# Attention in units of 256 query rows on 64-row array tiles, ahead of a mixture-of-experts block

## The chip, the cores and the metric

The kernel runs on one core of a Trainium2 chip. The metric is the device time of one execution in microseconds (us), as the median of several runs. Five engines take part: TensorE (PE in the profile, with its weight loads as PEld), VectorE (DVE), ScalarE (ACT), GpSimd (POOL) and SyncE (SP), which here only issues DMAs. SBUF is the working memory with 128 partitions; PSUM takes what TensorE writes, in 8 banks of 2 KB per partition.

## The reference

```
# q, k, v: (4 batches, 8 heads, 576 positions, 64)
scores = q @ k.T / 8
heads 0..3: position i sees i-31 .. i                      ("L", local)
heads 4..7: position i sees every j <= i with j % 32 == i % 32   ("S", strided)
attn = exp(scores - max); attn /= attn.sum() + 1e-9
x = attn @ v                        # 2304 tokens x 512
e = argmax(x @ w_gate); weight = softmax probability of e
x = weight * (relu(x @ w1[e]) @ w2[e])   # 8 experts, 512 -> 1024 -> 512
y = silu(x @ w_in) @ w_out          # 512 -> 2048 -> 512
```

All inputs and the output are float32.

## The kernel before

The order of the work is written out by hand (`manual_schedule`): every engine takes its instructions in program order, and SyncE's DMAs too stand in that order.

**Attention** goes in units of up to 128 query rows, 11 per batch and 44 in all. An L unit has four tiles of 32 positions; each sees 64 keys, its own 32 and the 32 before. An S unit has two groups; a group is three residue classes of 18 positions, 54 rows padded to 64, and sees its own 54 keys. Each unit takes all four heads of its kind at once, as two pairs (`pr`). The two heads of a pair lie on partitions 0-63 and 64-127 of `q`. So that one matmul over all 128 partitions gives both heads, `kL`, `kS`, `vL` and `vS` have a doubled layout with zero blocks: head 0's keys stand in one half of the columns with zeros beneath, head 1's in the other half. GpSimd and VectorE write these zeros once for both sets of input buffers (`zeros`), and the data are loaded by one DMA for each half, onto 64 (or 54) partitions (`halves`, `loadL`, `loadS`).

A unit goes through these steps: `s_qk` adds a mask (L245, bf16 against an identity) and then the scores into one PSUM bank (L251 for L, 128x32 stationary and 128 columns; L258 for S, 128x64 and 108 columns; a float32 matmul stands in the trace as two MATMUL and two LDWEIGHTS records); `s_max`, `s_sub` (DVE), `s_exp` (ACT), `s_sum`, `s_eps`, reciprocal (DVE), `s_norm` (POOL multiplies P by the reciprocals); `s_tr` transposes the normalised P (L312) and copies it (ACT L316); `s_pv` multiplies by the values (L329), copies to `xr` (ACT L336) and writes `xr` to the DRAM buffer `xg` (SP L339, L345); `s_xt` transposes `xr` (L362) and copies it to `xT` (ACT L365, L371; one copy for each S group). Scores, transposes, and transposed outputs have two PSUM buffers each.

The main loop interleaves these steps: iteration i does `s_qk(i)`, `s_tr(i-3)`, `s_pv(i-4)`, `s_xt(i-5)`. When a batch has gone through `s_xt`, its gate goes into `extra`, one piece at a time: two times `g_l4` (L381), `g_lg` (L395), and small steps on DVE (`g_oh`).

**Input loads.** There are two sets of input buffers. Batch b+2 is loaded when batch b's L units, and later its S units, have been through `s_pv`; these issues stand on SP's queue among the writes to `xg`.

**Routing** follows the last gate: prefix sums on TensorE, a chain of small DVE steps, a permutation by matmuls (L598), then the first gather of rows from `xg`, and from there the experts (L828, L850) and the last MLP (L828, L920). Expert weights are loaded in the order of the experts' sizes (`raw`, L702), so their first load is issued when the routing has the order.

Of the kernel before, what the change touches and what calls it, by code (L numbers as in the profile page):

```python
# [37 lines left out]
def _constants():  # L38
# [10 lines left out]
    ok0[:32, :32] = False  # L49
    parts["mL0"] = np.where(ok0, 0, NEG).astype(f)  # L50
    parts["mL"] = np.where(ok, 0, NEG).astype(f)
    q = p % 64
    c = np.arange(54)
    oks = (q[:, None] // 18 == c[None, :] // 18) & (c[None, :] % 18 <= q[:, None] % 18)
    oks[q >= 54, 0] = True
# [32 lines left out]
def _program(nc, tc, top, order, qL, kL, vL, qS, kS, vS, wg, cst, wE, wM, out):  # L88
# [16 lines left out]
    with ExitStack() as ctx:  # L105
        io = ctx.enter_context(tc.tile_pool(name="io", bufs=1))
        cp = ctx.enter_context(tc.tile_pool(name="cp", bufs=1))
        wk = ctx.enter_context(tc.tile_pool(name="wk", bufs=4))
        psS = ctx.enter_context(tc.tile_pool(name="psS", bufs=2, space=PSUM))
        psT = ctx.enter_context(tc.tile_pool(name="psT", bufs=2, space=PSUM))  # L110
        psR = ctx.enter_context(tc.tile_pool(name="psR", bufs=1, space=PSUM))
        psX = ctx.enter_context(tc.tile_pool(name="psX", bufs=2, space=PSUM))
        psM = ctx.enter_context(tc.tile_pool(name="psM", bufs=1, space=PSUM))
# [3 lines left out]
        def C(n):  # L117
# [6 lines left out]
        mb = {n: cp.tile([128, 4, OFF[n][1]], BF16, name="b" + n) for n in ("mL", "mL0", "mS")}  # L124
# [6 lines left out]
        L4 = cp.tile([128, NT], F32, name="L4")  # L131

        shp = dict(
            qL=[128, 2, 576], kL=[128, 2, 2, 608], vL=[128, 2, 18, 2, 64],
            qS=[128, 2, 608], kS=[128, 2, 2, 594], vS=[108, 2, 11, 2, 64],
        )
        ins = [{n: io.tile(shp[n], F32, name=f"{n}{i}") for n in shp} for i in range(2)]

        def loadL(b):
            d = ins[b % 2]  # L140
            nc.sync.dma_start(out=d["qL"], in_=qL[b])
            for i in range(2):
                nc.sync.dma_start(out=d["kL"][64 * i : 64 * i + 64, :, i, :], in_=kL[b, 64 * i : 64 * i + 64])
            for i in range(2):
                nc.sync.dma_start(out=d["vL"][64 * i : 64 * i + 64, i], in_=vL[b, i])

        def loadS(b):
            d = ins[b % 2]
            nc.sync.dma_start(out=d["qS"], in_=qS[b])
            for i in range(2):  # L150
                nc.sync.dma_start(out=d["kS"][64 * i : 64 * i + 64, :, i, :], in_=kS[b, 64 * i : 64 * i + 64])
            for i in range(2):
                nc.sync.dma_start(out=d["vS"][54 * i : 54 * i + 54, i], in_=vS[b, i])

        def zeros(i, n):
            for h in range(2):
                p = slice(64 * h, 64 * h + 64)
                if n == "vS":
                    yield from (ins[i][n][:, h, x : min(x + 4, 11)] for x in range(0, 11, 4))
                elif n == "vL":  # L160
                    yield from (ins[i][n][p, 1 - h, x : x + 3] for x in range(0, 18, 3))
                else:
                    yield from (ins[i][n][p, x, 1 - h, :] for x in range(2))

        def halves(n, src, m, by, lo, hi):
            for i in range(2):
                o = d0[n][m * i : m * i + m]
                if by:
                    nc.sync.dma_start(out=o[:, :, i, lo:hi], in_=src[0, m * i : m * i + m, :, lo:hi])
                else:  # L170
                    nc.sync.dma_start(out=o[:, i, lo:hi], in_=src[0, i, :, lo:hi])


        d0 = ins[0]
# [4 lines left out]
        def warm(n):  # L179
            wt = psS.tile([128, 512], F32, tag="S", name="wt")  # L180
            for _ in range(n):
                nc.tensor.matmul(wt, zw[:, :128], zw, start=True, stop=True)
# [4 lines left out]
        nc.sync.dma_start(out=d0["qL"][:, :, :128], in_=qL[0, :, :, :128])  # L187

        halves("kL", kL, 64, 1, 0, 288)
        nc.sync.dma_start(out=d0["qL"][:, :, 128:], in_=qL[0, :, :, 128:])  # L190
        halves("kL", kL, 64, 1, 288, 608)
        halves("vL", vL, 64, 0, 0, 12)
        for lo, hi in ((0, 336), (336, 608)):
            nc.sync.dma_start(out=d0["qS"][:, :, lo:hi], in_=qS[0, :, :, lo:hi])
            halves("kS", kS, 64, 1, lo, min(hi, 594))
            if lo == 0:
                halves("vL", vL, 64, 0, 12, 18)
        for z in zeros(0, "kL"):
            nc.gpsimd.memset(z, 0.0)
        nc.scalar.copy(idb, C("ident"))  # L200
        for n in ("mL0", "mL", "mS"):
            nc.scalar.copy(mb[n], C(n).unsqueeze(1).to_broadcast([128, 4, OFF[n][1]]))
        nc.scalar.copy(ident, C("ident"))
        for i, z in enumerate(zeros(0, "vL")):
            (nc.vector if i < 6 else nc.gpsimd).memset(z, 0.0)
        zl = [*zeros(0, "kS"), *zeros(1, "vS"), *zeros(1, "kL"), *zeros(1, "kS"), *zeros(1, "vL")]
        for z in zeros(0, "vS"):
            nc.vector.memset(z, 0.0)
        halves("vS", vS, 54, 0, 0, 11)
# [8 lines left out]
        for _ in range(6):  # L218
            nc.gpsimd.memset(zl.pop(0), 0.0)
# [98 lines left out]
        def s_pv(i):  # L318
# [27 lines left out]
            if b + 2 < B:  # L346
                if i % 11 == 4:
                    loadL(b + 2)
# [781 lines left out]
```

## Time and profile before

| | |
|---|---|
| median of 3 runs | 802.28 us (801.39 to 807.32) |
| profiled execution: its time | 804.88 us |
| its span, first to last instruction | 802.9 us |
| mean granted TensorE clock | 0.975 |
| PE / PEld / DVE / ACT / POOL busy | 760.1 / 664.8 / 437.7 / 350.2 / 214.9 us |

The busy shares are averages over two very different stages, the attention (up to about 125 us) and the experts with the MLP (from about 148 us), and have to be read by stage.

### The profile page before, as it was taken

What the parts mean: (1) busy time and instruction counts of PE and PEld (TensorE: products, weight loads), DVE (VectorE), ACT (ScalarE), POOL (GpSimd) and SP (SyncE); (2) the same over time, 40 slices, a digit from 0 to 9 for tenths busy, and PEclk for the clock granted to TensorE, in tenths of its full rate; (3) what the DMA queues carried; (4) which work ended last, traced back from release to release, by engine and by line L of the source; (5) the groups of instructions that cost most, each with busy time, mean ns of one, the idle gap of its engine ahead of it and who ended that gap; (6) DMA issues with size and microseconds to landing.
All of it is one profiled execution on the core that took longest, in us unless ns stands there. A gap on an engine that the chain in (4) does not pass through costs nothing.

```text
span 802.9 us, 13934 instructions
## 1 busy us (share of the span) xinstructions
PE 760.1 (95%) x4983; PEld 664.8 (83%) x4983; DVE 437.7 (55%) x979; ACT 350.2 (44%) x843; POOL 214.9 (27%) x272
## 2 busy tenths in 40 slices
PE   8788978899999999999999999999999999999996
PEld 4455644799988999999977899999999989999995
DVE  7444635775878888887899632232232233223221
ACT  4445644566656665674545432232232233223221
POOL 8412312653443444533366500010010000001001
PEclk8889988999999999999999999999999999999999
DMA  9986743866755856764222000010000000001001
GB/s 221 176 199 193 171 121 118 282 189 216 240 186 187 257 159 209 224 181 156 82 79 54 9 32 1 0 40 1 1 29 11 1 8 34 0 1 40 1 1 42
DMA packets 45309, 83.30 MB, mean 104 GB/s; under 512 B 7817, under 2 KB 14875, under 8 KB 44851
## 3 DMA queue, kind: packets, MB, share of 16 engines
q1 hardware_dynamic: 41896, 72.44, 31.9%
q0 software_dynamic: 3312, 9.91, 3.7%
q8 instruction: 41, 0.67, 0.4%
q14 instruction: 33, 0.27, 0.1%
q10 hardware_dynamic: 27, 0.01, 0.0%
HBM read 72.82 MB, written 9.52 MB: 103 GB/s over the span
## 4 chain that ended last, share of the span: by engine, by line
PE 69%; DVE 13%; DMA 10%; issue 4%; ACT 2%; POOL 1%; SPq 1%; ACTq 0%; POOLq 0%; DVEq 0%
PE hps L828 31%; PE acc L920 22%; PE acc L850 9%; DVE t L750 4%; DMA kS<-in_kS 3%; DMA vL<-in_vL 3%; DVE t L761 2%; DVE w L739 2%; PE XR L329 2%; DVE t L755 2%; DMA xg<-xr 1%; ACT w L738 1%; DMA raw<-in_wE 1%; DMA qS<-in_qS 1%; PE sc L258 1%
## 5 line engine op out<-in xcount | busy, mean ns | idle before, releaser
L828 PE MATMUL hps<-x,w 128*128 128x384 f32 (+7 forms) x1344 | 231.7, 321 | 6.1 <-DVE x L820 4.3
L828 PEld LDWEIGHTS hps<-x,w 128*128 128x128 f32 x1344 | 213.9, 188 | 13.2 <-DVE x L820 5.3
L936 DVE TENSOR_TENSOR g<-g,hps 128x384 f32<-128x384 f32 x96 | 53.1, 553 | 183.3 <-ACT g L935 183.3
L935 ACT ACTIVATE g<-hps 128x384 f32<-128x384 f32 x96 | 47.0, 490 | 179.0 <-PE hps L828 179.0
L850 PE MATMUL acc<-h,w 128*128 128x256 f32 (+7 forms) x768 | 120.0, 305 | 0.3 <-ACT yT L860 0.3
L850 PEld LDWEIGHTS acc<-h,w 128*128 128x128 f32 x768 | 112.5, 188 | 0.7 <-ACT yT L860 0.5
L920 PE MATMUL acc<-wm,h 128*128 128x512 f32 x432 | 109.1, 394 | 1.6 <-POOL h L938 1.6
L920 PE MATMUL acc<-w,h 128*128 128x512 f32 x432 | 107.0, 394 | 1.7 <-POOL h L938 1.7
L828 PE MATMUL hps<-x,wm 128*128 128x384 f32 x576 | 106.6, 336 | 0.0
L828 PEld LDWEIGHTS hps<-x,wm 128*128 128x128 f32 x576 | 101.8, 188 | 3.1
L949 POOL DMA_INDIRECT out<-ob,TI x18 | 17.6, 976 | 322.4 <-ACT ob L948 296.6
L920 PEld LDWEIGHTS acc<-w,h 128*128 128x128 f32 x432 | 80.2, 188 | 19.1 <-POOL h L938 3.8
L920 PEld LDWEIGHTS acc<-wm,h 128*128 128x128 f32 x432 | 80.0, 188 | 18.0 <-POOL h L938 3.7
L739 DVE TENSOR_TENSOR w<-raw,w 128x512 fp32r<-128x512 f32 x97 | 71.5, 765 | 29.9 <-ACT w L738 24.8
L937 ACT CAST h<-g 128x384 fp32r<-128x384 f32 x96 | 49.3, 513 | 66.7 <-DVE g L936 66.7
L738 ACT CAST w<-raw 128x512 fp32r<-128x512 f32 x128 | 73.0, 620 | 3.8 <-DVE nx L615 2.9
L938 DVE TENSOR_TENSOR h<-g,h 128x384 fp32r<-128x384 f32 x80 | 44.7, 559 | 46.3 <-ACT h L937 46.3
L739 POOL TENSOR_TENSOR w<-raw,w 128x512 fp32r<-128x512 f32 x31 | 44.5, 1436 | 26.2 <-ACT w L738 18.9
L269 DVE TENSOR_REDUCE mx<-sc 128x4 f32<-128x216 f32 (+3 forms) x44 | 17.5, 399 | 52.5 <-PE sc L258 34.3
L302 POOL TENSOR_TENSOR Pn<-P,rc 128x216 f32<-128x216 f32 (+3 forms) x43 | 24.8, 577 | 74.1 <-DVE rc L300 63.0
L777 POOL TENSOR_TENSOR wm<-raw,wm 128x256 fp32r<-128x256 f32 x32 | 24.0, 752 | 73.0 <-ACT wm L775 66.0
L750 DVE TENSOR_SCALAR t<-raw 128x256 uint32<-128x256 uint32 x64 | 42.6, 686 | 0.1
(151 smaller groups left out, 800.8 us busy)
## 6 DMA issues: line engine op xcount, KB each, us to landing
raw<-in_wE SPq DMA_DIRECT2D x128, 256.0 KB
raw<-in_wM SPq DMA_DIRECT2D x64, 256.0 KB
vL<-in_vL SPq DMA_DIRECT2D x6, 576.0 KB
vS<-in_vS SPq DMA_DIRECT2D x8, 297.0 KB
xg<-xr SPq DMA_DIRECT2D x40, 54.0 KB
xg<-xr SPq DMA_DIRECT2D x16, 128.0 KB
kL<-in_kL SPq DMA_DIRECT2D x6, 304.0 KB
qS<-in_qS SPq DMA_DIRECT2D x3, 608.0 KB
```

The lines of the kernel that those rows point to most:

```text
L302: (nc.gpsimd if i < N - 1 else nc.vector).tensor_tensor(out=v4(z["Pn"], r, w), in0=z["P"], in1=rc[:r].unsqueeze(2).to_broadcast([r, 4, w]) ...
L738: nc.scalar.copy(wh, raw)
L739: (nc.gpsimd if i % 4 == 0 and i != 8 else nc.vector).tensor_tensor(out=wl, in0=raw, in1=f32(wh), op=ALU.subtract)
L750: nc.vector.tensor_scalar(out=t, in0=hi, scalar1=3, scalar2=0x3FFFFFF8, op0=ALU.logical_shift_left, op1=ALU.bitwise_and,)
L777: nc.gpsimd.tensor_tensor(out=wl, in0=v, in1=f32(wh), op=ALU.subtract)
L828: nc.tensor.matmul(ps[:, :n], w[a][:, 128 * k : 128 * k + 128], xh[:, b, k, :n], start=i == 0, stop=i == 11)
L850: nc.tensor.matmul(acc[d][:, :n], w[a][:, 128 * d : 128 * d + 128], hc[:, b, :n], start=(f == 0 and a + b == 0), stop=(f == 7 and a == 1),)
L920: nc.tensor.matmul(acc[t], hc[:, a, 128 * t : 128 * t + 128], wt[b], start=(f == 0 and a + b == 0), stop=(f == 15 and a == 1),)
L935: nc.scalar.activation(g, ps[:, :n], AF.Sigmoid)
L936: nc.vector.tensor_tensor(out=g, in0=g, in1=ps[:, :n], op=ALU.mult)
L937: nc.scalar.copy(hc[:, 0, :n], g)
L938: (nc.gpsimd if first else nc.vector).tensor_tensor(out=hc[:, 1, :n], in0=g, in1=f32(hc[:, 0, :n]), op=ALU.subtract)
```

## The change

The unit is doubled: an L unit is eight tiles, an S unit four groups, 256 rows as two "columns" `s` of 128 rows; there are 9 L and 11 S units over all batches together, 20 in the order of a written list. The zero blocks and their memsets go. Each head has its own matmul on 64 array rows (`tile_position=(64*r, ...)`), with 64 score columns or 65 value columns; the two heads of a pair write to two PSUM banks (`sc[:, r]`, `X[:, r]`). The values get a column of ones, so that the sum of P comes out of `s_pv` as column 64; `s_sum` goes, P is transposed without being normalised, and `s_norm` (now on DVE, out of PSUM) normalises the result instead. K and V are loaded onto 128 partitions by one DMA each; there are three sets of input buffers. Scores, transposes, values' products and transposed outputs have one PSUM buffer each (the first and third of two banks), the gate has two. `xr` has 6 buffers instead of 14. The two zero writes to `tabd` go from SP's queue to GpSimd's. Routing, experts and MLP are the same, apart from which PSUM pools the routing uses.

```diff
-        wk = ctx.enter_context(tc.tile_pool(name="wk", bufs=4))
-        psS = ctx.enter_context(tc.tile_pool(name="psS", bufs=2, space=PSUM))
-        psT = ctx.enter_context(tc.tile_pool(name="psT", bufs=2, space=PSUM))
+        wk = ctx.enter_context(tc.tile_pool(name="wk", bufs=3))
+        psS = ctx.enter_context(tc.tile_pool(name="psS", bufs=1, space=PSUM))
         psR = ctx.enter_context(tc.tile_pool(name="psR", bufs=1, space=PSUM))
-        psX = ctx.enter_context(tc.tile_pool(name="psX", bufs=2, space=PSUM))
-        psM = ctx.enter_context(tc.tile_pool(name="psM", bufs=1, space=PSUM))
+        psT = ctx.enter_context(tc.tile_pool(name="psT", bufs=1, space=PSUM))
+        psX = ctx.enter_context(tc.tile_pool(name="psX", bufs=1, space=PSUM))
+        psM = ctx.enter_context(tc.tile_pool(name="psM", bufs=2, space=PSUM))
...
-            qL=[128, 2, 576], kL=[128, 2, 2, 608], vL=[128, 2, 18, 2, 64],
-            qS=[128, 2, 608], kS=[128, 2, 2, 594], vS=[108, 2, 11, 2, 64],
+            qL=[128, 2, 576], kL=[128, 2, 608], vL=[128, 18, 2, 65],
+            qS=[128, 2, 608], kS=[128, 2, 608], vS=[128, 11, 2, 65],
...
+        def load(b, n, lo=0, hi=None):
+            if n[0] == "v":
+                nc.sync.dma_start(out=ins[b % 3][n][:, lo:hi], in_=src[n][b, :, lo:hi])
+            else:
+                nc.sync.dma_start(out=ins[b % 3][n][:, :, lo:hi], in_=src[n][b, :, :, lo:hi])
...
+        load(0, "qL", 0, 256)
+        load(0, "kL", 0, 288)
+        load(0, "vL", 0, 8)
+        load(0, "qL", 256, 576)
+        load(0, "kL", 288, 608)
+        load(0, "vL", 8, 18)
+        load(0, "qS", 0, 280)
+        load(0, "kS", 0, 280)
+        load(0, "vS")
+        load(0, "qS", 280, 608)
+        load(0, "kS", 280, 608)
...
+        units = [("L", 0), ("L", 8), ("S", 0), ("S", 4), ("L", 16), ("S", 8)]
+        units += [("L", 24), ("L", 32), ("S", 12), ("S", 16), ("S", 20)]
+        units += [("L", 40), ("L", 48), ("S", 24), ("S", 28), ("S", 32)]
+        units += [("L", 56), ("L", 64), ("S", 36), ("S", 40)]
+        later = {
+            0: [(1, "qS"), (1, "kS"), (1, "vS")],
+            1: [(2, "qL"), (2, "kL"), (2, "vL")],
+            3: [(2, "qS"), (2, "kS"), (2, "vS")],
+            5: [(3, "qL"), (3, "kL"), (3, "vL")],
+            6: [(3, "qS"), (3, "kS"), (3, "vS")],
+        }
         N = len(units)
         st = {}
+        def parts(i):
+            ty, at = units[i]
+            if ty == "L":
+                return [(s, k, 32, *divmod(at + 4 * s + k, 18)) for s in range(2) for k in range(4)]
+            return [(s, k, 64, *divmod(at + 2 * k + s, 11)) for s in range(2) for k in range(2)]
...
+            sc = psS.tile([128, 2, 512], F32, tag="S", name="sc")
+            ps = parts(i)
+            starts = {s: k for s, k, m, b, t in ps if t == 0}
+            if ty == "S":
+                masks = [("mS", 0, 4)]
+            elif starts:
+                masks = [(["mL0", "", "mL2"][starts[s]] if s in starts else "mL", 2 * s, 2) for s in range(2)]
+            else:
+                masks = [("mL", 0, 4)]
+            for r in range(2):
+                for j, (m, c, n) in enumerate(masks):
+                    nc.tensor.matmul(
+                        sc[:, r, 64 * c : 64 * (c + n)].rearrange("p (a w) -> p a w", w=64), idb,
+                        mb[m].unsqueeze(1).to_broadcast([128, n, 64]), start=j == 0, stop=False,
+                    )
+            for s in range(2):
+                for pr in range(2):
+                    for s_, k, m, b, t in ps:
+                        if s_ != s:
+                            continue
+                        d = ins[b % 3]
+                        for r in range(2):
+                            h = slice(64 * r, 64 * r + 64)
+                            if ty == "L":
+                                q = d["qL"][h, pr, 32 * t : 32 * t + 32]
+                                kk = d["kL"][h, pr, 32 * t : 32 * t + 64]
+                            else:
+                                q = d["qS"][h, pr, 54 * t : 54 * t + 64]
+                                kk = d["kS"][h, pr, 54 * t : 54 * t + 64]
+                            c = 64 * (2 * s + pr)
+                            nc.tensor.matmul(
+                                sc[m * k : m * k + m, r, c : c + 64], q, kk,
+                                start=False, stop=s + pr == 2, tile_position=(64 * r, m * k),
+                            )
+            st[i] = dict(S=sc[:, :, :256].rearrange("p r (c w) -> p r c w", w=64))
...
+            z["D"] = wk.tile([128, 4, 2, 64], F32, tag="D", name="D")
             nc.vector.tensor_tensor(
+                out=z["D"].rearrange("p c r w -> p r c w"), in0=z["S"],
+                in1=z["mx"].unsqueeze(3).to_broadcast([128, 2, 4, 64]), op=ALU.subtract,
             )
         def s_exp(i):
             z = st[i]
+            z["P"] = wk.tile([128, 4, 128], F32, tag="P", name="P")
+            nc.scalar.activation(z["P"], z["D"].rearrange("p c r w -> p c (r w)"), AF.Exp, scale=0.125)
...
+        def s_tr(i):
             z = st[i]
+            z["T"] = psT.tile([128, 4, 128], F32, tag="T", name="T")
+            for c in range(4):
+                nc.tensor.transpose(z["T"][:, c, :], z["P"][:, c, :], ident)
+        def s_pt(i):
+            z = st[i]
+            z["PT"] = wk.tile([128, 4, 128], F32, tag="PT", name="PT")
+            nc.scalar.copy(z["PT"], z["T"])
+        def s_pv(i):
+            z = st[i]
+            ty, _ = units[i]
+            X = psR.tile([128, 2, 512], F32, tag="R", name="XR")
+            z["X"] = X[:, :, :260].rearrange("p r (c w) -> p r c w", w=65)
+            for s in range(2):
+                for pr in range(2):
+                    for s_, k, m, b, t in parts(i):
+                        if s_ != s:
+                            continue
+                        V = ins[b % 3]["v" + ty]
+                        for r in range(2):
+                            h = slice(64 * r, 64 * r + 64)
+                            c = 2 * s + pr
+                            nc.tensor.matmul(
+                                X[m * k : m * k + m, r, 65 * c : 65 * c + 65],
+                                z["PT"][h, c, m * k : m * k + m], V[h, t, pr, :],
+                                start=True, stop=True, tile_position=(64 * r, m * k),
+                            )
         def s_eps(i):
             z = st[i]
+            z["rc"] = wk.tile([128, 2, 4], F32, tag="rc", name="rc")
+            nc.vector.tensor_scalar_add(z["rc"], z["X"][:, :, :, 64], 1e-9)
+            nc.vector.reciprocal(z["rc"], z["rc"])
         def s_norm(i):
             z = st[i]
+            xr = z["xr"] = wk.tile([128, 2, 256], F32, tag="xr", name="xr", bufs=6)
+            nc.vector.tensor_tensor(
+                out=xr.rearrange("p s (q r w) -> p r (s q) w", q=2, r=2), in0=z["X"][:, :, :, :64],
+                in1=z["rc"].unsqueeze(3).to_broadcast([128, 2, 4, 64]), op=ALU.mult,
+            )
+        def s_put(i):
+            xr = st[i]["xr"]
+            ty, at = units[i]
+            if ty == "L":
+                nc.sync.dma_start(
+                    out=xg[32 * at : 32 * at + 256, 0:256].rearrange("(s p) d -> p s d", s=2), in_=xr
+                )
+                return
+            for k in range(2):
+                rows = [(s, m, b, t) for s, k_, m, b, t in parts(i) if k_ == k]
+                for s, m, b, t in rows:
...
+            z["XX"] = psX.tile([128, 4, 128], F32, tag="X", name="XX")
+            for c in range(4):
                 nc.tensor.transpose(
+                    z["XX"][:, c, :], z["xr"][:, c // 2, 128 * (c % 2) : 128 * (c % 2) + 128], ident
...
+        for i in range(N + 3):
             def on(j):
                 return 0 <= j < N
+            if on(i - 2):
+                s_eps(i - 2)
+                s_norm(i - 2)
+                s_put(i - 2)
             if on(i):
                 s_qk(i)
+            more()
+            if on(i - 1):
+                s_tr(i - 1)
+                s_pt(i - 1)
+            if on(i):
                 s_max(i)
+            more()
+            if on(i - 2):
+                s_xx(i - 2)
+            more()
             if on(i - 1):
+                s_pv(i - 1)
             if on(i):
                 s_sub(i)
+            more()
+            if on(i - 2):
+                s_xt(i - 2)
             if on(i):
                 s_exp(i)
+            for a in later.get(i, ()):
+                load(*a)
+            more(2)
```

## Rows read from the trace of the kernel before

**Rows 1.** Windows: length, busy us (instructions) per engine, granted clock, DMA share, GB/s.

```profile
0.00:44.00 44.00, 34.75 (x394) 20.05 (x394) 28.02 (x90) 20.76 (x65) 27.14 (x62) 0.84 0.96 196
125.00:148.00 23.00, 17.37 (x122) 9.65 (x122) 15.70 (x67) 8.88 (x27) 7.37 (x6) 0.85 0.52 163
148.00:803.00 655.00, 636.71 (x3636) 590.65 (x3634) 355.86 (x652) 276.61 (x609) 161.13 (x159) 1.00 0.28 88
```

**Rows 2.** Chain that ended last, to the first expert matmul: start, duration, what.

```profile
5.94 6.70 DMA vL<-in_vL
...
35.05 11.36 DMA kS<-in_kS
...
94.10 9.04 DMA qS<-in_qS
...
125.47 1.54 PE l L381 x16
...
147.64 4.51 PE hps L828 x36
```

**Rows 3.** The same chain: gate matmuls, then one unit's steps on TensorE.

```profile
78.09 0.96 PE l L381 x8
...
80.34 1.21 PE lg L395 x10
...
91.85 0.37 PE XX L362 x2
92.22 0.11 PE sc L245
92.33 0.57 PE sc L251 x16
92.91 0.36 PE T L312 x2
93.27 0.59 PE XR L329 x8
```

**Rows 4.** Windows: qS moving; kS and vS moving; only writes to xg.

```profile
67.00:68.00 1.00, 1.00 (x15) 0.76 (x13) 0.91 (x3) 0.50 (x3) 0.24 (x1) 1.00 1.01 363
69.00:72.00 3.00, 3.00 (x37) 1.81 (x36) 2.25 (x8) 1.96 (x7) 0.85 (x2) 1.00 0.94 235
...
111.00:115.00 4.00, 4.00 (x60) 2.84 (x61) 2.44 (x13) 1.94 (x7) 0.55 (x1) 1.00 0.22 66
```

**Rows 5.** Windows of L251 alone: PE busy (matmuls in flight), PEld, clock, DMA.

```profile
92.26:92.28 0.02, 0.02 (x3) 0.02 (x3) 1.00 0.00 0
92.28:92.30 0.02, 0.02 (x4) 0.02 (x6) 1.00 0.36 103
...
92.40:92.42 0.02, 0.02 (x8) 0.02 (x7) 1.00 0.00 0
```

**Rows 6.** The same for L329 of an S unit.

```profile
93.21:93.23 0.02, 0.02 (x2) 0.02 (x2) 1.00 0.19 51
93.37:93.39 0.02, 0.02 (x4) 0.02 (x4) 1.00 0.32 102
```

**Rows 7.** Groups by line and form up to 170 us: busy, mean ns, idle before.

```profile
L371 ACT COPY xT<-XX 128x108 f32<-128x108 f32 x40 | 10.6, 370 | 0.0
...
L251 PEld LDWEIGHTS sc<-kL,qL 128*32 128x32 f32 x288 | 8.6, 119 | 11.8 <-DMA xg<-xr 5.4 <-issue 3.6 <-POOL CUM L215 1.4
...
L295 DVE TENSOR_SCALAR rc<-sm 128x4 f32<-128x4 f32 x36 | 7.8, 216 | 0.0
...
L820 DVE TENSOR_TENSOR x<-xt,x 128x512 fp32r<-128x512 f32 x4 | 2.6, 670 | 1.0 <-ACT x L819 1.0
...
L819 ACT CAST x<-xt 128x512 fp32r<-128x512 f32 x4 | 2.2, 579 | 3.5 <-issue 3.5
```

**Rows 8.** Timeline of TensorE: the first score matmuls.

```profile
6.20 0.65 PE L251 MATMUL sc<-kL,qL 128*32 128x128 f32 x16 [1.07 <-DMA kL<-in_kL]
```

**Rows 9.** Window after a stall of TensorE: the granted clock.

```profile
47.00:51.00 4.00, 4.00 (x40) 1.59 (x36) 1.24 (x5) 1.43 (x4) 0.61 (x1) 0.50 1.01 216
```

More of the change, by code (lines that the diff above doesn't have):

```diff
@@ L131, in _program @@
         L4 = cp.tile([128, NT], F32, name="L4")
+        xT = cp.tile([128, 4, NT], F32, name="xT")
         shp = dict(
-            qL=[128, 2, 576], kL=[128, 2, 2, 608], vL=[128, 2, 18, 2, 64],
-            qS=[128, 2, 608], kS=[128, 2, 2, 594], vS=[108, 2, 11, 2, 64],
-        )
[L137 to L163, printed above, removed]
@@ L175, in _program @@
+        src = dict(qL=qL, kL=kL, vL=vL, qS=qS, kS=kS, vS=vS)
+        ins = [{n: io.tile(shp[n], F32, name=f"{n}{i}") for n in shp} for i in range(3)]
+        def load(b, n, lo=0, hi=None):
[3 more added lines that the diff above has]
+                nc.sync.dma_start(out=ins[b % 3][n][:, :, lo:hi], in_=src[n][b, :, :, lo:hi])
         zw = cp.tile([128, 512], BF16, name="zw")
@@ L186, in _program @@
         nc.sync.dma_start(out=cs[:, :nf], in_=cst[:, :nf])
[L187 to L199, printed above, removed]
-        nc.scalar.copy(idb, C("ident"))
[L201 to L209, printed above, removed]
+        load(0, "qL", 0, 256)
[9 more added lines that the diff above has]
+        load(0, "kS", 280, 608)
+        nc.scalar.copy(idb, C("ident"))
+        for n in ("mL0", "mL", "mS", "mL2"):
+            nc.scalar.copy(mb[n], C(n))
+        nc.gpsimd.tensor_copy(ident, C("ident"))
+        for n in ("qL", "kL", "vL"):
+            load(1, n)
         nc.sync.dma_start(out=cs[:, nf:], in_=cst[:, nf:])
         nc.sync.dma_start(out=wgs, in_=wg)
-        loadL(1)
         nc.gpsimd.memset(onb, 1.0)
@@ L215, in _program @@
         nc.gpsimd.memset(CUM[:, 0, :], 0.0)
[L216 to L228 removed]
+        nc.gpsimd.dma_start(out=tabd[0:PADF], in_=zt[:PADF])
@@ L352, in first_loads @@
-        def first_loads(i):
-            if i == 5:
-                loadS(1)
+        done = {"L": 0, "S": 0}
+        gated = [0]
         def s_xt(i):
             z = st.pop(i)
-            b, ty, t, n = units[i]
-            r = z["R"]
-            X = psX.tile([128, 2, 128], F32, tag="X", name="XX")
-            for pr in range(2):
-                nc.tensor.transpose(X[:, pr, :r], z["xr"][:r, 128 * pr : 128 * pr + 128], ident[:r, :r])
-            xT = xTs[b]
+            ty, at = units[i]
```

221 lines of the change are left out of this document (55 added, 166 removed).

## The prediction

> **What bounds the kernel now.** I read the windows by stage first [rows 1]. From 148 us on TensorE is busy 637 of 655 us at the full clock (granted 1.00, the 2.4 GHz level): experts and MLP are bound by TensorE, and the change leaves them alone. From 125 to 148 us runs the routing, a serial chain that starts at the last batch's gate, and it too stays. So the question is when the last gate starts: at 125.47 us now, and the first expert matmul follows at 147.64 [rows 2]. Whatever the attention gains comes out at the end one to one, as the first expert weights are requested by the routing's result and no attention buffer holds them up.
>
> Next comes the chain of waits up to there [rows 2]. Until 46 us it is made of input loads (kS from 35.05 lasts 11.36 us), and it meets qS again at 94.10 for 9.04 us. In the first 44 us the DMA engines are busy 0.96 of the time and deliver only 196 GB/s [rows 1]. Between these waits TensorE sets the pace: one unit takes .37 + .11 + .57 + .36 + .59 = 2.0 us [rows 3]. So the attention has two limits, the loads and TensorE, and the change touches both.
>
> **Loads.** With qS (128 partitions in one DMA) in motion the engines deliver 363 GB/s at full share; with kS and vS (64 and 54 partitions to a DMA) it is 235 at a share of .94 [rows 4]. After the change all loads have 128 partitions, so the bounds are 235 and 363. I take 330, near the row of the like shape. The amounts: per batch q 0.59 and 0.62 MB, k 0.62 each, vL 1.20, vS 0.73, together 4.4 MB, 17.8 MB with constants (zero blocks were never loaded, so bytes don't fall). A unit writes 0.26 MB to xg; alone, writes moved 66 GB/s at a share of .22, that is 300 at full share [rows 4].
>
> Where does TensorE wait? Unit 5 ("S", 8) is the first that needs batch 1's S data. Ahead of its scores stand 0.3 (constants) + 4.4 + 2.4 + 1.24 = 8.34 MB, 25.3 us at 330 GB/s, with an allowance of 2 us for the first issues and 0.8 MB of writes (2.6 us): 29.9 us. Later needs (unit 10, unit 15) come by the same sum some us ahead of their use. On SP's queue the writes of results now stand behind loads that wait for a free buffer or for the queue; `xr` has six buffers, so a write may be some five iterations (18 us) late before VectorE's normalisation, and with it TensorE, waits. I cost this at nothing; with slow loads it belongs to rival D.
>
> **TensorE.** The float32 matmuls are seen starting in groups: for L, four are in flight by 92.30, eight by 92.40 [rows 5], one group for each .11 us, four column tiles abreast; for S two abreast at about the same period [rows 6]. 16 records make four groups, .43 us, which with .14 of start and drain is the .57 of the chain [rows 3]. In the new units a matmul streams 64 or 65 columns instead of 108 or 128, so a group should take .055, but there are twice as many: 64 records (L) or 32 (S) in each of scores and values for 256 rows. No row shows two 64-row halves of the array at work together. If they do run together, eight (L) or four (S) are abreast and the streaming x is 8 x .055 = .44 us; if they add nothing, 16 x .055 = .88, which is what two units of before have. Weight loads count double also: one lasts 119 ns [rows 7], longer than a 55 ns matmul. A tile that loads one set while it works with the other then takes about (119 + 55) / 2 = 87 ns for a matmul, 8 x 87 = .70 us on eight tiles. S loads 64 columns at a time. I take x = .8.
>
> An iteration is then masks 2 x .11, four transposes .72, four more .74, twice the .15 around a segment, and 2x: 1.98 + 2x = 3.58 us, against 4.0 for two units of before. The other engines stay below it. VectorE: max, subtract and normalise with 512 elements each (.67 by L820 [rows 7]), two small steps (.2 each): 2.4. ScalarE: exponential and copy at .58 (L819), four copies for S at .37 (L371): 2.6. GpSimd loses its memsets and multiplications, which no chain row of before names, so this is worth nothing by itself. The single PSUM buffer for the scores costs nothing either: `s_qk(i+1)` waits for `s_sub(i)`, 1.4 us of VectorE, under the transposes and the values' matmuls (2.5 us) on TensorE; only the first iteration has nothing to cover it.
>
> **The sum.** Start as now, 6.2 us [rows 8] (fewer but larger first pieces). 20 iterations x 3.58 = 71.6. Three gates in between, each .96 + .96 + 1.2 = 3 [rows 3]: 9. Unit 5 could start at 6.2 + 5 x 3.58 = 24.1 and waits until 29.9: 5.8. After such a wait TensorE ran at half clock: at 47 to 51 us the granted clock was .50, the 1.2 GHz level, after it had idled [rows 9]; 3 us for that. Behind the last iteration the last unit still needs transposes .72, copy .58, values .95, reciprocal .4, normalisation .67, transposes .74, four copies 1.48, and some 10 hand-overs: 6.3. Together 101.9 us instead of 125.5, a gain of 23.6. The profiled span of 802.9 becomes 779.3 and its execution of 804.88 becomes 781.3; against the median of 802.28, which lies 2.6 lower, I predict 779.
>
> **Rivals.** A, *both halves abreast in full*: x = .44, the iteration 2.86, 57.2 for all; unit 5 would be ready at 20.5 and waits 9.4. Attention ends at 91: 768. For it: groups of four start within .04 us [rows 5]. Against it: the weight loads' length.
>
> B, *a price for each matmul whatever its width*: 16 matmuls now start within .4 us, 25 ns apart. If that is a floor, L costs 64 x 25 = 1.6 a segment and S .8; 9 x 5.18 + 11 x 3.58 = 86, the wait shrinks to 1: end at 108.5, time 785. Against it: three to four in flight within .04 us [rows 5], so starts stand closer together than 25 ns where tiles differ. The Trainium skill, in "TensorE: Matmul & The Clock Gate", Part 1, "Wait — 56ns, not 53.3ns?", states this floor of about 25 ns from start to start; here the rows contradict it across tiles. "TensorEngine Tiling (Array Packing)", "Instruction Overhead", speaks against the change too: one should not take a tiling factor from a dimension that is small already; no run here shows such narrow tiles yet.
>
> C, the other side, *weight loads that are not hidden*: the gate's second matmuls have 8 columns, so their weight loads stand bare: 1.21 / 10 = 121 ns for 128 columns [rows 3], 30 for 32, 60 for 64. If each 64-row load holds up its matmuls so, x = 64 x 30 ns = 1.94 for L and the same for S; iteration 5.86, all 117; no wait on loads is left, end at 139: 815, slower. It decides from x = 1.6 (25 ns for an L matmul, 50 for S), where 20 x 5.2 + 21.5 reaches 125.5. Against it: by 92.30 six loads are in flight beside four matmuls [rows 5]. For it: twice the loads for half the work each.
>
> D, *loads don't get faster*: at 235 GB/s batch 3's S data, needed by unit 15, are there at 17.8 MB / 235 = 75.7, + 11.4 (writes) + 2 = 89; five iterations, a gate and the tail make 116: 793. For it: the 54-partition and 64-partition rows mix with writes. Against: 363 GB/s with qS.
>
> That the change doesn't do what it says would show as x = .88 with loads as predicted: 782, inside the forecast.
>
> **How the numbers follow.** A measurement of this kernel can tell about 1% from no change: below 794 is faster, above 810 slower. Forecast 48% (772 to 787 with x between .6 and .95), A 14%, B 15%, C 12%, D 11%. The range leaves out C and the lower edge of A: 768 to 798. Faster: forecast, A, B and some over half of D less a margin for the unseen, .81; slower: most of C, .10; the rest, .09, between.
>
> **What would show it.** Right: in the windows, loads above 300 GB/s at full share in the first 40 us; one stall of TensorE near 25 to 30 us; iterations of 3.6 us; the last gate near 102 us; routing 22 us long as now. Matmul groups of L with more than four abreast speak for A; L iterations well longer than S ones for B; PEld busy without a gap through the scores and values for C. The forecast falls if TensorE is found waiting for VectorE or ScalarE in each iteration, if writes late on SP's queue hold up the normalisation, or if small matmuls leave the granted clock at .50.

## The result, and the profile after

The changed kernel takes 783.32 us (median of 4, 782.61 to 784.15), the kernel before 804.1 in the runs beside it (801.39 to 807.32): the ratio of the two is 0.974, its 95% interval 0.9696 to 0.9784. The prediction was 779, its range 768 to 798. The profiled execution took 783.98 us, its span 782.0.

Windows by stage (columns as in [rows 1]) of the changed kernel:

```profile
10.00:15.00 5.00, 0.00 (x0) 0.00 (x0) 0.00 (x0) 0.00 (x0) 0.00 (x0) 0.50 0.97 80
...
20.00:30.00 10.00, 7.44 (x196) 5.49 (x179) 3.50 (x8) 1.78 (x4) 0.00 (x0) 0.56 1.03 412
30.00:45.00 15.00, 9.95 (x325) 7.51 (x322) 7.22 (x15) 5.26 (x15) 0.84 (x2) 0.92 1.02 402
...
104.00:128.00 24.00, 16.89 (x115) 10.52 (x116) 16.63 (x68) 9.14 (x26) 7.28 (x6) 0.86 0.60 181
128.00:782.00 654.00, 636.08 (x3635) 590.48 (x3633) 355.75 (x651) 275.80 (x607) 159.75 (x159) 1.00 0.28 87
```

The experts' stage is the same to 0.6 us in TensorE's busy time (636.08 here, 636.71 in [rows 1]). The loads run at 400 to 412 GB/s from 20 to 45 us, where the kernel before had 196 in its first 44 us [rows 1]. But from 10 to 15 us no engine does anything, while the DMA engines are full and move 80 GB/s.

Chain that ended last (start, duration, what), with a steady stretch of an S and an L iteration:

```profile
3.91 12.67 DMA kL<-in_kL
...
40.16 2.76 issue
...
81.10 0.32 PE sc L226 x2
81.42 0.62 PE sc L245 x32
82.04 0.60 PE T L273 x4
...
82.73 0.59 ACT PT L278
...
83.36 0.70 PE XR L295 x32
84.06 0.33 PE sc L226 x2
84.39 0.84 PE sc L245 x53
...
87.56 0.79 PE sc L245 x53
...
104.39 1.17 PE l L372 x12
...
127.75 2.33 PE hps L812 x19
```

The chain reaches the last gate at 104.39 (125.47 in [rows 2]) and the experts at 127.75 (147.64), so the attention gives 21.1 us and the routing, 23.4 us long instead of 22.2, takes 1.2 back. (104.39 is where the last twelve of the gate's sixteen records begin; the other four begin at 103.40. Before, all sixteen stand together.) What the routing lost lies in its last steps on TensorE, from 124.31 on: they take 1.94 + 1.49 us at a mean granted clock of .55, close to the 1.2 GHz level, against 1.07 + .76 us at 1.00 before. By the end of the span the gain is 20.9 us (802.9 - 782.0). The S iteration from 81.10 to 84.06 takes 2.96 us and the next, up to the following mask at 87.24, 3.18; the forecast was 3.6. With steps that much faster, the last gate should have come before the forecast 101.9, not after it. The timeline of TensorE says where the rest went (the bracket holds the idle time ahead of the line and its releaser):

```profile
16.71 1.17 PE L245 MATMUL sc<-kL,qL 64*32 64x64 f32 x64 [7.75 <-DMA kL<-in_kL]
23.46 0.92 PE L245 MATMUL sc<-kS,qS 64*64 64x64 f32 x24 [1.70 <-issue]
29.82 0.33 PE L245 MATMUL sc<-kS,qS 64*64 64x64 f32 x4 [0.86 <-issue]
36.37 0.68 PE L295 MATMUL XR<-vS,PT 64*64 64x65 f32 x27 [1.46 <-issue]
42.92 0.43 PE L295 MATMUL XR<-vL,PT 64*32 64x65 f32 x6 [2.76 <-issue]
58.38 0.39 PE L385 MATMUL lg<-cs,L 128*128 128x8 f32 x2 [1.75 <-issue]
```

First a wait of 7.75 us of the second unit for its keys, a piece that was issued at 3.91 us. Then five gaps, 8.5 us together, each in the middle of a run of matmuls that had already begun. No semaphore ended them, which the profile calls "issue".

### The profile page after: what moved, and what is told of

Its sections match the earlier page's. It is cut to its first block, busy times and chain, and to the rows that moved or that the text cites. A ratio compares the mean times of both kernels' runs of the same rounds, so it can differ in the third digit from the quotient of the medians.

```text
span 782.0 us, 15274 instructions
## 1 busy us (share of the span) xinstructions
PE 730.9 (93%) x5897; PEld 657.3 (84%) x5899; DVE 423.9 (54%) x846; ACT 325.2 (42%) x738; POOL 173.2 (22%) x194
## 4 chain that ended last, share of the span: by engine, by line
PE 75%; DVE 11%; issue 5%; DMA 3%; ACT 2%; POOL 1%; SPq 0%; POOLq 0%; ACTq 0%; DVEq 0%
PE hps L812 32%; PE acc L904 22%; PE acc L834 11%; DVE t L734 3%; PE XR L295 2%; PE sc L245 2%; PE T L273 2%; DMA kL<-in_kL 2%; DMA raw<-in_wE 2%; DVE t L745 2%; DVE w L723 2%; DVE t L739 1%; ACT PT L278 1%; ACT w L722 1%; PE sc L226 1%
## 5 line engine op out<-in xcount | busy, mean ns | idle before, releaser
L761 POOL TENSOR_TENSOR wm<-raw,wm 128x256 fp32r<-128x256 f32 x32 | 24.2, 757 | 72.6 <-ACT wm L759 64.5
L750 DVE SCALAR_TENSOR_TENSOR raw<-m,t 128x256 f32<-128x256 bf16 x64 | 36.6, 592 | 1.2
L759 ACT CAST wm<-raw 128x256 fp32r<-128x256 f32 x32 | 13.0, 406 | 57.9 <-DVE raw L750 57.9
```

The costliest lines, as they stand in the source:

```text
L750: nc.vector.scalar_tensor_tensor(out=v, in0=m, scalar=TINY * TINY, in1=t.bitcast(F32), op0=ALU.is_ge, op1=ALU.mult)
L761: nc.gpsimd.tensor_tensor(out=wl, in0=v, in1=f32(wh), op=ALU.subtract)
```

## The experiments

Four theories: T1, the 7.75 us wait comes from the two zero writes to `tabd`, 224 rows of 4 bytes from 96 and 128 partitions, which the change put ahead on GpSimd's queue; T2, most of the gain is the loads' 128 partitions to a DMA; T3, the two halves of the array work abreast, and that is why the steps are shorter than forecast; T4, the gaps without a releaser come with the load traffic. One expectation has a T5: what the steps alone are worth in the kernel before. Rivals are named in each expectation. In the results, ratio and interval are those of the time to the kernel before. First what TensorE's steps are worth by themselves, then the waits.

**Heads in turn** (T3). All matmuls of the lower 64 rows first, then all of the upper, in scores and values:

```diff
-            for s in range(2):
+            for r_ in range(2):
+              for s in range(2):
...
-                        for r in range(2):
+                        for r in (r_,):
```

> The changed kernel with the order of the score and value matmuls changed: first all of the lower 64 array rows, then all of the upper, instead of the two in turn. Theory T3: the halves run together only when neighbours in the order lie on different halves; the 32 score records of an S unit then take .85 to .95 us instead of .62, the 64 of an L unit about .95 instead of .82 to .9; time 789 to 795. Rival: a matmul has a fixed price of about 10 ns (L) to 14 ns (S) whatever lies beside it, and the order means nothing: 783.

788.28 us (784.85 to 789.62), ratio 0.9774, interval 0.9743 to 0.9804. The chain of waits in this run, an S unit's scores and values and an L unit's scores:

```profile
83.31 0.33 PE sc L226 x2
83.63 0.91 PE sc L246 x30
...
85.22 0.59 ACT PT L279
85.86 0.98 PE XR L297 x30
...
87.16 0.92 PE sc L246 x60
```

The same 32 records (the chain counts 30 of them here) take .91 instead of .62 for the scores and .98 instead of .70 for the values; L's scores take .92 instead of .79 to .84. So the halves do work abreast when their matmuls alternate, nearly in full for S (.91 less .15 around it is .76; .62 less .15 is .47, and fully abreast would be .44) and only in part for L. One thing is not parted by this run: the two halves write to two PSUM banks, so matmuls that alternate between the halves alternate between the banks too. With that said, T3 holds in its mechanism. The time is just below the 789 to 795 expected of it. The trace gives a reason: beside the slower steps the gaps are 3.2 us together, where the changed kernel has 8.5.

**One batch loaded, the kernel before.** Only batch 0 is loaded, and all batches compute on its operands, so the output is another; only the time up to the last gate is read, since the experts then get other shares of the tokens.

```diff
-        loadL(1)
...
-            d = ins[b % 2]
+            d = ins[0]
...
-                if i % 11 == 4:
-                    loadL(b + 2)
-                if i % 11 == 10:
-                    loadS(b + 2)
+                pass
...
-            if i == 5:
-                loadS(1)
+            pass
```

> The kernel before in which only batch 0 is loaded and all 44 units compute on it (wrong output in batches 1 to 3, the end longer as experts overflow; only the time up to the last gate is read). Theory T5: without waits for loads TensorE's pace of 2.0 us a unit puts the last gate at 100 to 108 us, where the changed kernel with one batch has it at 94; so about 10 us of the change's work is in TensorE's steps. Rival: both come at the same time, 92 to 96, and the steps are worth nothing.

TensorE's timeline has the last gate at

```profile
103.16 1.61 PE L376 MATMUL l<-xT,wgs 128*32 128x288 f32 x16
```

as expected (100 to 108), and TensorE was busy all 80 us from 20 to 100. Of before's 125.47 us, 103.2 are steps and start, 22.3 waiting for loads and what follows from it.

**One batch loaded, the changed kernel.** The same edit there (also another output).

> The changed kernel in which only batch 0 is loaded and all 20 units compute on it (wrong output in batches 1 to 3; experts may then be fuller than their places and the end longer, so only the time up to the last gate is read). Theory T4: TensorE's gaps within a row of matmuls that nothing in the profile releases (1.7, .9, 1.5, 2.8 and 1.75 us, between 21 and 58 us) come from input loads that fill the DMA engines; without loads after 17 us they are gone (under 1 us in all), and so are the waits for data: after the first 17 us the last gate comes within some 65 us, at 80 to 85 us. Rival: the gaps are the price of twice as many TensorE instructions and stay: last gate at 88 to 95 us.

TensorE's timeline of this run:

```profile
16.92 1.17 PE L237 MATMUL sc<-kL,qL 64*32 64x64 f32 x64 [8.00 <-DMA kL<-in_kL]
24.31 0.92 PE L237 MATMUL sc<-kS,qS 64*64 64x64 f32 x24 [2.34 <-issue]
...
93.07 3.09 PE L364 MATMUL l<-xT,wgs 128*32 128x288 f32 x16
```

The last gate came at 93.07, not at T4's 80 to 85 but in the range that the rival had named, though not for the rival's reason, for the gaps did not stay: one of 2.34 us ended at 24.3 us, while batch 0 was still loading, and after it there were only two, of .20 and .36 us. T4 holds in this: the long gaps come with the traffic. The wait for the second unit's keys was 8.00 us as ever, so it has nothing to do with the later loads. It was still in the number, and the work behind it took 76 us and not the 65 that the expectation had reckoned.

**Zero writes late** (T1):

```diff
-        nc.gpsimd.dma_start(out=tabd[0:PADF], in_=zt[:PADF])
-        nc.gpsimd.dma_start(out=tabd[YC:TROWS], in_=zt[: TROWS - YC])
...
+            if i == 15:
+                nc.gpsimd.dma_start(out=tabd[0:PADF], in_=zt[:PADF])
+                nc.gpsimd.dma_start(out=tabd[YC:TROWS], in_=zt[: TROWS - YC])
```

> The changed kernel with one edit: the two writes of zeros to tabd (96 and 128 elements of 4 bytes), which GpSimd issues at 4.1 and 4.8 us, are issued in iteration 15. Theory T1: these writes are what slows every DMA between 10 and 16 us (33 to 73 GB/s there, second kL piece landing only at 16.7); without them the second unit's scores start by 9.5 us instead of 16.7, and the time falls by 5 to 8 us, to 775 to 778. Rival: the slow stretch belongs to the row-cut first pieces of the inputs (runs of 1.1 to 1.3 KB); then it stays where it is and the time stays at 783.

782.76 us (779.51 to 783.38), ratio 0.9702, interval 0.9676 to 0.9727: the expected time (775 to 778) was missed. Windows of this run:

```profile
10.00:15.00 5.00, 3.56 (x134) 2.75 (x134) 1.49 (x3) 1.11 (x2) 0.00 (x0) 0.50 1.03 389
...
65.00:68.00 3.00, 1.86 (x69) 1.37 (x63) 1.84 (x3) 0.58 (x1) 0.00 (x0) 1.00 0.22 11
68.00:72.00 4.00, 2.69 (x44) 1.13 (x43) 1.06 (x3) 1.40 (x6) 0.00 (x0) 0.67 0.24 54
```

Without the zeros the DMA engines move 389 GB/s from 10 to 15 us (80 before), and the second unit starts at 10.76. But where the zeros now stand, the engines move 11 GB/s from 65 to 68 us. And TensorE stops there, in the middle of a unit's values, though no load runs:

```profile
69.31 1.38 PE L293 MATMUL XR<-vL,PT 64*32 64x65 f32 x34 [2.16 <-issue]
```

The DMA view, 64.5 to 65 us of this run, has the queue that carries instructions (packets, MB, share of 16 engines):

```profile
q8 instruction: 1, 0.02, 50.9%
```

A packet here is one transfer of the queue, with a block of instructions in it. 50.9% of 16 engines' .5 us is 4.1 us for the one packet that began in this window, so it ended at 68.6 to 69.1, just ahead of TensorE's start at 69.31. In the changed kernel's windows such a packet takes 12 to 15%, .9 to 1.2 us. So the cause was right and the remedy no remedy: the writes had only been moved under TensorE's instructions. T4 had to be put more sharply: the gaps are waits for instructions, which **Four more matmuls** below puts to the test.

**Zeros as two runs** (T1 again). The same zeros at the old place, from one partition, as two runs of 384 and 512 bytes:

```diff
-        zt = cp.tile([128, 1], I32, name="zt")
+        zt = cp.tile([1, 128], I32, name="zt")
...
-        nc.gpsimd.dma_start(out=tabd[0:PADF], in_=zt[:PADF])
+        nc.gpsimd.dma_start(out=tabd[0:PADF].rearrange("(a b) v -> a (b v)", a=1), in_=zt[:, :PADF])
```

(and the same for the second write)

> The changed kernel with the zeros for tabd written as two runs of 384 and 512 bytes from one partition instead of 96 and 128 pieces of 4 bytes from as many partitions; place and queue as they are. Theory T1: the pieces of 4 bytes hold up all DMA, TensorE's instructions too; then the slow stretch from 10 to 16 us is gone without coming back elsewhere (as it did near 65 to 69 us with the zeros late), the second unit's scores start by 10 us, time 774 to 778. Rival: any such write early on GpSimd's queue does it, whatever its pieces: 783.

778.05 us (777.57 to 780.48), ratio 0.9681, interval 0.9649 to 0.9712: 5.3 us by the medians. Its windows have no slow stretch any more:

```profile
10.00:15.00 5.00, 3.60 (x134) 2.75 (x134) 1.53 (x3) 1.11 (x2) 0.00 (x0) 0.50 1.04 385
15.00:20.00 5.00, 3.28 (x42) 2.60 (x40) 2.30 (x5) 0.51 (x1) 0.00 (x0) 0.50 1.03 414
```

and TensorE's timeline has the second unit six us earlier; below it stands the last gate:

```profile
10.73 1.17 PE L245 MATMUL sc<-kL,qL 64*32 64x64 f32 x64 [2.31 <-DMA kL<-in_kL]
...
97.89 1.17 PE L372 MATMUL l<-xT,wgs 128*32 128x288 f32 x12 [0.32 <-ACT xT L353]
```

So 5.4 of the 7.75 us of waiting were the zeros'; 2.31 are left, and the unit starts .7 us later than expected. The last gate comes at 97.89 instead of 104.39. T1 is shown by the pair: late, the stretch moves with the writes; as two runs, it is gone.

**The same in the kernel before.** There the writes stood at 23.8 and 24.5 us on SP's queue.

> The kernel before with the zeros for tabd written as two runs from one partition. Theory T1 for the kernel before: its slow stretch (43 to 100 GB/s from 37 to 41 us) comes from the same pieces, issued at 24 us behind a full queue; without it 3 to 6 us are gained, 798 to 802 against 804 to 806. Rival: there the stretch is the load of vS over nine of sixteen engines, and nothing changes.

802.53 us (799.12 to 805.1), ratio 0.9975, interval 0.9952 to 0.9997, last gate 121.58 instead of 125.47. The slow stretch is gone here too: from 37 to 41 us the engines move 181 GB/s instead of 69. So the kernel before paid for the zeros as well, but by the medians only some 2 us, less than the 3 to 6 expected and at the edge of what can be told from nothing. That TensorE was waiting for other loads in any case is the likely reason, not a shown one.

**One batch, zeros as two runs**, in the changed kernel (another output):

> Zeros as two runs, and only batch 0 loaded: all four batches compute on batch 0's operands, so the output is another and the stages after the routing are not comparable; the first gate of batch 3 is what is read. Theory that what is left between the forecast and the stages is loads (the wait for the second unit's operands, TensorE gaps beside the loads): with both taken away the last gate starts at 84 to 88, since twenty iterations at 2.97 and 3.2 are 62, three gates 7.5, start and tail 12.6, and the gaps that stay beside batch 0's own loads 2 to 5; before's program with one batch loaded had its last gate at 103.16. Rival, that the gaps come whatever is loaded: 93 or more.

A window of this run:

```profile
20.00:30.00 10.00, 9.17 (x352) 7.34 (x336) 7.10 (x15) 5.74 (x17) 0.00 (x0) 0.95 0.16 47
```

and the last gate in TensorE's timeline:

```profile
85.82 2.11 PE L364 MATMUL l<-xT,wgs 128*32 128x288 f32 x12 [0.30 <-ACT xT L345]
```

As expected (84 to 88). Now the sums stand: before 103.2 of steps and 22.3 for loads; after 85.8 of steps, 97.89 - 85.82 = 12.1 for loads, 104.39 - 97.89 = 6.5 for the zeros. The change gains 17.3 in the steps and 10.2 in the loads and gives 6.5 back. Two of these are rough. Counted from the gate's first record (84.83 here) the steps are worth 18.3. And the 22.3 of the kernel before holds its own zeros, 2 us by the medians and 3.9 by the two profiles above, so the loads' share is rather 6 to 8 us and the zeros' 3 to 5.

**K and V in halves** (T2). The loads of k and v as two DMAs of 64 partitions, everything else as changed:

```diff
+            for h in range(1 if n[0] == "q" else 2):
+                p = slice(None) if n[0] == "q" else slice(64 * h, 64 * h + 64)
...
+                    nc.sync.dma_start(out=ins[b % 3][n][p, lo:hi], in_=src[n][b, p, lo:hi])
```

> The changed kernel with each load of kL, kS, vL and vS cut into two DMAs of 64 partitions, as before; bytes and layout are the same. Theory T2: 64 partitions to a DMA is what held the loads at 235 GB/s before; from 20 to 45 us the rate falls from 400-430 GB/s to 240-300, TensorE waits longer for units 4 to 8, time 788 to 796. Rival: the rate depends on bytes per row or on the mix with writes, not on the partitions of one DMA; rate and time stay (783).

806.85 us (803.71 to 808.77), ratio 1.0014, interval 0.9995 to 1.0033: nothing of the gain is left, more than T2 had asked for. Windows:

```profile
20.00:30.00 10.00, 6.56 (x122) 4.65 (x124) 3.39 (x8) 1.70 (x3) 0.00 (x0) 1.00 1.05 239
30.00:45.00 15.00, 9.58 (x196) 7.43 (x192) 4.89 (x10) 3.50 (x9) 0.84 (x2) 0.88 1.03 234
```

TensorE's timeline:

```profile
24.75 0.92 PE L247 MATMUL sc<-kS,qS 64*64 64x64 f32 x24 [1.31 <-issue]
...
58.82 1.09 PE L247 MATMUL sc<-kL,qL 64*32 64x64 f32 x53 [3.72 <-issue]
...
127.08 1.16 PE L374 MATMUL l<-xT,wgs 128*32 128x288 f32 x12 [0.31 <-ACT xT L355]
```

234 to 239 GB/s against 402 to 412, and the last gate at 127.08. The 17.3 us of shorter steps are worth nothing while the loads set the end: the two parts of the change are no sum. The other half, faster loads with the old steps, was not run; the kernel before with one batch bounds it at 22.3 us. The edit also halves the size of each DMA. Size is an unlikely reason: with the zeros as two runs, the loads from 10 to 15 us are in part pieces of 280 and 328 KB, on 128 partitions, and the rate is 385 GB/s.

**Loads spread** (T4). To the zeros as two runs, batches 1 to 3 are loaded in ten smaller portions, at iterations 0 to 10 instead of five at 0 to 6:

```diff
-            0: [(1, "qS"), (1, "kS"), (1, "vS")],
-            1: [(2, "qL"), (2, "kL"), (2, "vL")],
+            0: [(1, "qS"), (1, "kS")],
+            1: [(1, "vS")],
+            2: [(2, "qL"), (2, "kL")],
+            3: [(2, "vL")],
```

(and so on)

> The kernel with the zeros in one row and, besides, the loads of batches 1 to 3 (from batch 1's S data on) issued in ten smaller portions, one for most iterations from 0 to 10, instead of five portions in iterations 0, 1, 3, 5 and 6. Theory T4: TensorE's unexplained gaps (some 9 us in all) come where loads keep the DMA engines full for long; spread out, less than 5 us of them is left, and the time is 3 to 6 us below the kernel with the zeros alone, 769 to 774. Rival: the gaps go with the number of instructions and stay, or the later loads bring waits of their own: 775 to 780.

777.63 us (776.13 to 778.98), ratio 0.9671, interval 0.9643 to 0.9699; the gaps are 1.48, 1.58, .46, 2.22, 1.51 and .57 us, 7.8 together. Not as expected: the gaps are hardly fewer (9.1 with the zeros alone), and there is no gain that can be told from none. The portions still filled the DMA engines up to 36 us.

**Four more matmuls** (T4). If a gap is a wait for the next packet of instructions, its place is counted in instructions. Two things in the changed kernel's trace say so. From the end of one gap to the start of the next, the windows have 126 + 127, 125 + 125 and 127 + 126 matmul and weight-load records, and 380 + 380, three times as many, in the last:

```profile
23.46:28.96 5.50, 5.50 (x126) 4.32 (x127) 2.44 (x5) 1.70 (x3) 0.00 (x0) 0.51 1.02 414
29.82:34.91 5.09, 4.55 (x125) 3.61 (x125) 3.81 (x7) 2.57 (x7) 0.84 (x2) 1.00 1.02 411
36.37:40.16 3.79, 3.49 (x127) 2.74 (x126) 2.35 (x5) 1.48 (x6) 0.00 (x0) 1.00 1.02 399
42.92:56.63 13.71, 13.42 (x380) 9.87 (x380) 7.89 (x18) 5.98 (x14) 0.00 (x0) 0.77 0.76 261
```

And the instruction queue's section of its page has 48 packets for TensorE's 11,796 records, 246 to a packet (before: 41 for 9,966, 243 to a packet):

```profile
q8 instruction: 48, 0.79, 0.4%
```

So four matmuls were put into the first unit (with the zeros as two runs), written over by the masks behind them:

```diff
+            for r in range(4 if i == 0 else 0):
+                nc.tensor.matmul(sc[:, r % 2, 0:128], idb, idb, start=True, stop=True)
```

> The zeros as two runs, and four more matmuls in the first unit, which write to the score banks ahead of the masks and are written over by them. They shift every later TensorE instruction by four matmuls with their weight loads. Theory that the TensorE gaps which nothing in the profile releases are waits for the next packet of its instructions: each gap moves forward in the program by eight instructions, that is four score or value records: in the third unit's scores 28 of 32 records are left behind the gap instead of 24, in the fourth's 8 instead of 4, in its values 31 instead of 27, in the next L values 10 instead of 6. Rival, that they come from the data or the loads at a place of the program: the counts stay 24, 4, 27 and 6. The time should be that of the run with the zeros as two runs within a us.

One run, 776.41 us, from which no difference in time can be read. TensorE's timeline of it:

```profile
16.98 1.12 PE L247 MATMUL sc<-kS,qS 64*64 64x64 f32 x28 [1.52 <-issue]
23.52 0.34 PE L247 MATMUL sc<-kS,qS 64*64 64x64 f32 x8 [1.58 <-issue]
29.95 0.69 PE L297 MATMUL XR<-vS,PT 64*64 64x65 f32 x31 [0.41 <-issue]
36.15 0.33 PE L297 MATMUL XR<-vL,PT 64*32 64x65 f32 x10 [2.46 <-issue]
```

28, 8, 31 and 10 records are left behind the gaps instead of 24, 4, 27 and 6: each gap moved by the eight instructions added. In every other run of the changed program the first gap left 24, wherever it fell between 16 and 25 us. The packets' own times agree. In the changed kernel the one ahead of the gap that ends at 23.46 began between 21 and 21.5 us:

```profile
q8 instruction: 1, 0.02, 12.7%
```

That is 1.0 us, so it had landed by 22.5. The trace's records of the five gaps' packets have them landed at 22.06, 28.61, 35.02, 41.42 and 57.03 us, and TensorE went on 1.2 to 1.5 us after each. Shown: the gaps stand at the borders of TensorE's instruction packets.

**Eight buffers for `xr`.** The last chain of waits has a normalisation that waits 1.12 us for a write of `xr` at 100.88, which the prediction had costed at nothing. To the zeros as two runs:

```diff
-            xr = z["xr"] = wk.tile([128, 2, 256], F32, tag="xr", name="xr", bufs=6)
+            xr = z["xr"] = wk.tile([128, 2, 256], F32, tag="xr", name="xr", bufs=8)
```

> The zeros as two runs, and eight buffers for the normalised tile xr instead of six. In the run with the zeros as two runs and six buffers the last normalisation but the final one waited 1.12 us for a transfer of xr into xg (94.37 to 95.50), on the chain that leads to the last gate at 97.89. Theory that this wait is on the path: the last gate at about 96.8, and the median at about 777 against 778.05, 776 to 778. Rival, that the wait only hides another (the reciprocals, the X buffers or TensorE's own supply of instructions are as late): no change, 778 to 779.

778.51 us (776.12 to 778.86), ratio 0.966, interval 0.9637 to 0.9683. The time is that of six buffers, though from the time alone a gain below a us would not be seen: one gap near 50 us was 2.70 instead of 1.62 us in this run. The chain decides it. The wait is gone from it, and yet from the second last unit's values to the last gate it takes 6.18 us (91.41 to 97.59), with six buffers 6.19 (91.70 to 97.89): where the wait was, the last unit's values and their reciprocals now stand. The rival holds.

The best version is the changed kernel with the zeros as two runs, 778.05 us; the loads spread or eight buffers for `xr` add nothing that can be told from none.

## Why the prediction was right, and where it was not

The time and the sign were right and so was the place: all of the gain lies ahead of the last gate, 21.1 us there and 20.9 at the end. But the sum, 101.9 against 104.39, came out close because two errors met, dearer waits and cheaper steps. That much of it was luck.

- *x = .8, the streaming of a segment, was mis-sized.* The chain shows .62 for S's scores (x = .47, all but the bound of .44 for halves fully abreast) and .79 to .84 for L's (x = .64 to .69). The reckoning by the weight load's time, (119 + 55) / 2, was too dear. An S iteration is .32 + .60 + .71 + .62 + .70 = 2.95 us (.71 from the end of the transposes to the values, in which the other four transposes lie and the wait for ScalarE's copy): the masks are .10 longer than costed, the transposes .12 shorter, the segments 1.32 against 1.90. Rival A's mechanism is there, for S nearly in full; its price of 768 was not, since what A saves in steps the waits took.
- *Rival B's floor is not there.* 64 records in .84 less .15 are 11 ns apart, 32 in .47 are 15. The sentence of the Trainium skill that the prediction weighed ("TensorE: Matmul & The Clock Gate", Part 1, "Wait — 56ns, not 53.3ns?"), some 25 ns from start to start, does not hold across array tiles here. Rival C is ruled out by the same numbers. What is left of B is that L iterations are .2 us longer than S ones, 3.18 to 2.96.
- *The other engines stay below it* holds only in part. TensorE waits for ScalarE's copy of the transposes ahead of the values in 12 of the 20 iterations, mostly .24 to .30 us. Such a wait in each iteration was to be a sign against the forecast. In the steady stretch it lies inside the .71 above, .03 below the .74 costed for the second four transposes, so the sum did not suffer. The line, from the view of what waited for what, has the total, the number and the longest:

```profile
PE XR L295 <- ACT PT L278: 3.9, 12, 0.7
```

- *The gates* take 2.2 to 2.5 us on the chain, not 3.
- *Loads at 330 GB/s* were 400 to 412, above both bounds. T2's run showed what that is worth: with 234 to 239 the whole gain is lost. Rival D had priced this at 793, and it measured 806.85. D had left out the gaps, which slow loads lengthen: 19.5 us together in that run, the longest 4.08.
- *One stall of 5.8 us at unit 5 near 24 to 30 us* is the step that failed. Unit 5 doesn't wait for its data. The second unit waits 7.75 us at 9 to 16.7, and the cause of 5.4 of them is an edit that the prediction does not mention: two small DMAs that moved from SP's queue to the front of GpSimd's. What 224 single 4-byte writes do to the 16 engines was no term of the sum.
- *Gaps in TensorE's instructions*, 8.5 us, were no term of the sum. Neither did before's rows warn of them: there the scores' weight loads have 3.6 us of "issue" in 288 [rows 7], and none of TensorE's matmuls up to the last gate has such a gap. The change puts more instructions into less time, 4,302 matmul and weight-load records up to 104 us against 2,458 up to 125 us.
- *The clock*: .50, the 1.2 GHz level, from 10 us on and .56 on the mean of 20 to 30, behind the idle stretch; and .50 again from 43 to 49 us, behind the gap of 2.76 us. 3 us were allowed. Of the 12.1 us that loads still cost in the version with the zeros as two runs, the gaps are 7.9 (9.1, against 1.2 with one batch). The other 4 go with a lower clock (.89 on the mean of 20 to 60 us, against .99 with one batch), but no run shows the clock alone.

By terms: the run with one batch and the zeros as two runs has 85.82, of which 2.2 + 1.2 are waits; so steps, start and tail are some 82 us against the forecast's 93.1, although a stretch at a clock of .54 from 10 to 20 us is still in them. The rest of the changed kernel's 104.39, waits, gaps and the clock behind them, is 22 against 8.8.

## What to carry to other kernels

A DMA that writes many single words has a price even if nothing waits for it. Write it as a few runs, and look at GB/s, not at the share of busy engines, for the stretch where it lies. When a change gives TensorE many small matmuls in place of few, count its instructions per us as a load of their own, which shares the DMA engines with the data. And before adding up a faster step and a faster load, ask which of them hides the other: here the faster steps, with the loads slow, were worth nothing.

## What was not expected of the hardware

- While 224 4-byte rows from 96 and 128 partitions were written, the 16 DMA engines moved 80 GB/s for 5 us at a share of .97 (in another place 11 GB/s at .22 for 3 us); with the same bytes as two runs the slow stretch is not there (385 GB/s).
- The same matmuls take .62 us when they alternate between the two 64-row halves (and two PSUM banks) and .91 when one half comes after the other.
- TensorE's instructions come in packets of some 16 KB (0.79 MB in 48), about 250 matmul and weight-load records. At a border it stood still for up to 2.8 us while loads filled the DMA engines, up to 4.1 us with the slower loads, and for 2.16 us when the packet itself took 4.1 us. A packet's own time under the loads is no longer than without them (.9 to 1.2 us). In the changed kernel TensorE went on 1.2 to 1.5 us after the packet had landed, so much of each gap lies behind the packet; what happens in that time, and what holds the packet back before it, stays open.
